# A recurrent attention loop with one PSUM bank for values and weighted values instead of two, and a fifth half-pair of weights kept in PSUM

## Chip, cores and metric

One NeuronCore of a Trainium2 chip. The time is the device time of one execution in microseconds; a lower one is better. Weights, activations and outputs are bf16 and matrix products accumulate in f32.

## What is computed

Two independent parts share a kernel and their outputs are put side by side. Part A is a gated long convolution (shift filter, FFT convolution over 2048 positions, gate). Part B is attention with a recurrent memory, and it takes most of the time:

```python
mem = mem0                                   # 8 rows
for s in range(n_seg):                       # 64 segments of 32 rows
    h = concat([mem, x[s*32:(s+1)*32]])      # 40 rows x 1024
    q, k, v = h @ Wq, h @ Wk, h @ Wv         # 32 heads of 128
    p = softmax(where(mask, q @ k.T * scale, -1e9))
    o = (p @ v) @ Wo                         # 40 rows x 1024
    mem = o[:8]                              # next segment's memory
    outs.append(o[8:])
```

Each segment needs the one before it, because its first eight rows are that one's result. `Wq`, `Wk`, `Wv` and `Wo` are 1024 x 4096 (or the reverse) each, 32 MB in all, and every segment uses every weight once.

## The kernel before

**Where weights are.** The weights are cut into 64 pairs of 512 KB, a pair being two tiles of 128 x 1024: 8 pairs of q and k in each of four groups of eight heads (`("qk", g, i)`), 4 of v and 4 of the output projection o. Most pairs are resident in SBUF for the whole loop. Two are "parked" in PSUM (`PARKED`): four banks hold their four tiles, and in each segment ACT copies one tile and DVE the other into a buffer of the ring (`unpark`, lines 715 to 719). The other 17 (`STREAM`) are copied once into DRAM tiles `Wst` in a convenient layout and then read anew in every segment. They go through `wring`, a ring of five buffers of 512 KB. `done` (line 724) is called behind the last product with a pair; it hands the freed buffer to the next pair of the list, either by a DMA that SP issues (`place`, line 707) or by an entry on the list of copies out of PSUM. SP issues in program order, so a load waits until PE has finished with the buffer, and the loads behind it wait too.

**PSUM.** A bank is 2 KB in each of 128 partitions. During the loop four of the eight banks hold parked weights, one (`ps_qk`) takes the sums of q and k and later those of the output, two (`ps_acc`) take in turn the sums of v (`vacc`), the weighted values (`otacc`), the transposed `x` and a filler, and one (`ps_ts`) takes the transposed q and k, the scores and the transposed memory.

**A segment.** Line 906 starts the loop. For each group g from 0 to 3: `qk_part` multiplies 32 rows (eight of memory and 24 of `x`; the last eight of every segment's `x` do not depend on the memory and were multiplied before the loop) by eight chunks of q and k weights, each chunk four matmuls of 512 columns side by side in four column strips of the array. `scores` and `softmax` belong to the group before (g - 1), and `pv` (lines 836 to 856), the weighted values, to the one before that (g - 2). `pv` has four parts c, each with four small matmuls that use 32 rows of the array (tile position 32c), one PSUM bank, and a cast by ACT from that bank into `OT` (line 851). It is called for two parts at a time. Then `qk_out` casts q and k on ACT, `v_part` multiplies by the v weights, `tr_a` transposes q and k, and `v_out` casts v. After the four groups, the output products `wo` follow (eight steps of four matmuls for each group), with group 3's softmax and the weighted values of groups 2 and 3 between them, the transposition of the next segment's `x` (`h_rows`) and at last `Y_sb`, an ACT cast of the output. `fill_mem` transposes its first eight rows into the next `hT`, and the next segment starts.

**Queues around it.** ACT works in order: copies out of PSUM, the casts, the exponentials and, in group 2, the issue of the load of the next `x` rows, `H` (line 661). `H` shares its buffer with `Y_sb`, so that load waits until the stores of `Y_sb`, which POOL issues, have landed. DVE does the row maxima, the normalisation and the copies of transposed q and k. POOL copies the last eight rows of `OT` into `OL`, issues the stores of `OL` and `Y_sb`, and the loads of `VB`, the values made before the loop. Semaphores are placed by the framework; the order of instructions on each engine is the order of the program, written out by hand.

After the loop, the last stage (lines 969 on) multiplies the collected rows `OLs` by the output weights. In the last segment, the streamed o pairs are loaded into SBUF places that are no longer needed (lines 911 to 915).

Of the kernel before, what the change touches and what calls it, by code (L numbers as in the profile page):

```python
# [21 lines left out]
def fused_kernel(ctx: ExitStack, tc, q, k, v, shift_k, ssm_k, ssm_D, outa, x, mem0, Wq, Wk, Wv, Wo, outb, n_seg):  # L22
# [15 lines left out]
    scale = 128.0 ** -0.5  # L38
    RING = 5
    STREAM = {"qk": ((2, 5), (3,), (2, 6), (2, 6)), "v": ((0, 3), (1,), (2,), (2,)), "o": ((2,), (1,), (0, 3), (2,))}  # L40
    PARKED = {("qk", 0, 2): ("v", 0, 1), ("v", 0, 3): ("qk", 1, 6)}

    msched = tc.manual_schedule()
# [13 lines left out]
    streamed = [key for key in pairs if key[2] in STREAM[key[0]][key[1]]]  # L57
    parked = list(PARKED.values())
    resident = [key for key in pairs if key not in streamed and key not in parked]
    Wst = {key: dram.tile([128, 2, 1024], BF, name=f"Wst{key[0]}{key[1]}_{key[2]}") for key in streamed}  # L60

    def half_src(key, n):
        m, g, i = key
# [51 lines left out]
    def relay(n):  # L115

        for _ in range(n):
            if relaid:
                key = relaid.pop(0)
                for i in range(2):  # L120
                    nc.gpsimd.dma_start(Wst[key][:, i, :], half_src(key, i))

    relaid = list(streamed)
# [540 lines left out]
    H = load_h(0)  # L664


    ps_park = cw_.enter_context(tc.tile_pool(name="b_ps_park", bufs=1, space=PSUM))
    park = {key: [ps_park.tile([128, 1024], BF, name=f"park{key[1]}_{n}") for n in range(2)] for key in parked}

    park_s = stv.tile([128, 4, 1024], BF, tag="stv", name="park_s")  # L670
    halves = [(key, n) for key in parked for n in range(2)]
    assert rows.at >= 160
    rows.load_to(96)
    park_w = []
# [8 lines left out]
    for i, (key, n) in enumerate(halves):  # L683
        tw = ps_p.tile([128, 1024], BF, tag="pp", name="park_t")
        for c in range(8):
            nc.tensor.transpose(tw[:, c * 128:(c + 1) * 128], park_w[i][:, c * 128:(c + 1) * 128], ident[:])
        nc.vector.tensor_copy(park_s[:, i, :], tw[:])
        rows.half(2, "AD")
        for c in range(8):
            nc.tensor.transpose(park[key][n][:, c * 128:(c + 1) * 128], park_s[:, i, c * 128:(c + 1) * 128], ident[:])  # L690
    while rows.at < 192:
        rows.half(2, "AD")
    assert len(rows.loaded) == 96
# [3 lines left out]

    pp = ExitStack()
    ps_qk = pp.enter_context(tc.tile_pool(name="b_ps_qk", bufs=1, space=PSUM))
    ps_acc = pp.enter_context(tc.tile_pool(name="b_ps_acc", bufs=2, space=PSUM))  # L700
    ps_ts = pp.enter_context(tc.tile_pool(name="b_ps_ts", bufs=1, space=PSUM))

    placed = {}
# [3 lines left out]
    def place():  # L707

        if todo:
            key = todo.pop(0)  # L710
            t = ring.tile([128, 2, 1024], BF, tag="wring", name="wring")
            nc.sync.dma_start(t[:], Wst[key][:])
            placed.setdefault(key, []).append((t[:, 0, :], t[:, 1, :]))

    def unpark():
        while to_copy:
            key, t = to_copy.pop(0)
            nc.scalar.copy(t[:, 0, :], park[key][0][:])  # L718
            nc.vector.tensor_copy(t[:, 1, :], park[key][1][:])

    def pair(key):
        return (res[key][:, 0, :], res[key][:, 1, :]) if key in res else placed[key].pop(0)
# [18 lines left out]
    def qk_part(u, kcs):  # L741
        if kcs[0] == 0:
            u.qk = ps_qk.tile([128, 512], F32, tag="qk", name="qkacc")
        for kc in kcs:
            w = pair(("qk", u.g, kc))
            for t in range(2):
                for c2 in range(2):
                    p0 = 32 * (2 * t + c2)
                    nc.tensor.matmul(u.qk[p0:p0 + 32, :], lhsT=hT[:, kc, :], rhs=w[t][:, c2 * 512:(c2 + 1) * 512],  # L749
                                     start=(kc == 0), stop=(kc == 7), tile_position=(0, p0))  # L750
            done(("qk", u.g, kc))
# [84 lines left out]
    def pv(u, s, cs, ts_bank=False):  # L836
        if cs[0] == 0:
            u.OT = act2.tile([128, 8, 40], BF, tag="OT", name="OT")
        PTv = u.PT[:].rearrange("p (a i) k q -> p i k a q", a=2)
        for c in cs:  # L840
            pool, tag = (ps_ts, "ts") if ts_bank and c == 2 else (ps_acc, "acc")
            ot = pool.tile([128, 512], F32, tag=tag, name="otacc")
            r = slice(32 * c, 32 * c + 32)
            for i in range(2):
                o = ot[:, 64 * i:64 * i + 64]
                nc.tensor.matmul(o, lhsT=u.v[r, i * 128:(i + 1) * 128], rhs=PTv[r, i, 0], start=True, stop=False,  # L846
                                 tile_position=(32 * c, 0))
                nc.tensor.matmul(o, lhsT=VB[r, i * 128:(i + 1) * 128], rhs=PTv[r, i, 1], start=False, stop=True,  # L848
                                 tile_position=(32 * c, 0))
            ov = ot[:, 0:128].rearrange("e (i q) -> e i q", i=2)  # L850
            nc.scalar.copy(u.OT[:, 2 * c:2 * c + 2, :], ov[:, :, 0:40])  # L851
        if cs[-1] == 3:
            to = OL[:] if s + 1 < n_seg else OLs[:, s]
            nc.gpsimd.tensor_copy(to[:, 8 * u.g:8 * u.g + 8, :], u.OT[:, :, 32:40])  # L854
            if u.g == 3 and s + 1 < n_seg:
                nc.gpsimd.dma_start(OLd[s], OL[:].rearrange("e h r -> e (h r)"))

    def wo(u, Y, hhs=range(8)):
        for hh in hhs:
            if hh % 2 == 0:  # L860
                w = pair(("o", u.g, hh // 2))
            for dq in range(4):
                nc.tensor.matmul(Y[32 * dq:32 * dq + 32, 0:256], lhsT=u.OT[:, hh, 0:32],  # L863
                                 rhs=w[hh % 2][:, dq * 256:(dq + 1) * 256],
                                 start=(u.g == 0 and hh == 0), stop=(u.g == 3 and hh == 7),
                                 tile_position=(0, 32 * dq))
            if hh % 2 == 1:
                done(("o", u.g, hh // 2))
# [37 lines left out]
    for s in range(n_seg):  # L906
        us = []
        for g in range(4):
            if g == 2 and s + 1 < n_seg:
                H = load_h(s + 1)  # L910
            if g == 2 and s + 1 == n_seg:
                spare = [key for key in resident if key[0] != "o" and key[1] < 2 and key not in early]
                for key, at in zip([key for key in streamed if key[0] == "o"], spare):
                    nc.sync.dma_start(res[at][:], Wst[key][:])
                    res[key] = res[at]
            u = nxt
            us.append(u)
            qk_part(u, range(0, 4))
            unpark()
            if g < 3:  # L920
                nxt = load_b(s, g + 1)
            elif s + 1 < n_seg:
                nxt = load_b(s + 1, 0)
            if g >= 1:
                S = scores(us[g - 1])
            if g >= 2:
                pv(us[g - 2], s, (0, 1))
            if g >= 1:
                softmax(us[g - 1], S)
            qk_part(u, range(4, 6))  # L930
            if g >= 2:
                pv(us[g - 2], s, (2, 3))
            qk_part(u, range(6, 8))
            qk_out(u)
            v_part(u, range(0, 8))
            tr_a(u)
            v_out(u)
            unpark()
            if g == 3 and s + 1 == n_seg:
                for s0, s1 in ((0, 32), (32, s)):  # L940
                    nc.sync.dma_start(OLs[:, s0:s1].rearrange("e s h r -> e s (h r)"),
                                      OLd[s0:s1].rearrange("s e x -> e s x"))
        Y = ps_qk.tile([128, 512], F32, tag="qk", name="yacc")
        wo(us[0], Y, range(0, 4))
        softmax(us[3], scores(us[3]))
        wo(us[0], Y, range(4, 8))
        pv(us[2], s, (0, 1))
        wo(us[1], Y, range(0, 4))
        pv(us[2], s, (2, 3))
        wo(us[1], Y, range(4, 8))  # L950
        if s + 1 < n_seg:
            hT = new_hT()
            h_rows(H, hT, 8)
        wo(us[2], Y)
        pv(us[3], s, (0, 1))
        pv(us[3], s, (2, 3), True)
        if s + 1 < n_seg:
            load_vb(s + 1)
        wo(us[3], Y)
        Y_sb = act.tile([128, 256], BF, tag="st", name="Y_sb")  # L960
        nc.scalar.copy(Y_sb[:], Y[:, 0:256])
        if s + 1 < n_seg:
            fill_mem(hT, Y_sb)
            idle = ps_acc.tile([128, 512], F32, tag="acc", name="idle")
            keep_warm(idle, 2)
        for dq in range(4):
            nc.gpsimd.dma_start(outb[32 * s:32 * s + 24, dq * 256:(dq + 1) * 256], Y_sb[32 * dq + 8:32 * dq + 32, :])

    pp.close()
    ps_l = cw_.enter_context(tc.tile_pool(name="b_ps_l", bufs=2, space=PSUM))  # L970
    outl = outb.rearrange("(s t) d -> t s d", t=32)
    for sh in range(2):
# [83 lines left out]
```

## Time and profile before

| What | Value |
|---|---|
| Median of 3 runs | 2201.1 us (2187.66 to 2211.53) |
| Profiled execution | 2200.53 us, span 2198.5 us |
| First and last `Y_sb` | 448.0 and 2137.0 us |
| Busy in the span | PE 1808.6, PEld (weight loads) 1028.8, DVE 1082.4, ACT 836.0, POOL 500.4 us |
| Moved in the span | 732.29 MB, mean 333 GB/s |
| Streamed loads, 512 KB each | q and k 448, v 320, o 315; 6.2 to 6.3 us from issue to landing |
| Granted TensorE clock | 0.96 of full speed |

PE is TensorE, ACT ScalarE, DVE VectorE, POOL GpSimd, SP SyncE. In the views, "L851" is a line of the kernel, `out<-in` are the names of the tiles, and an arrow behind an idle time names what ended it; "issue" there means that the engine waited for nothing that the profile shows. A row of the order of time merges equal instructions that follow each other: start, duration, engine, line, operation, names, shapes, count. The end of a matmul is modelled, since matmuls are pipelined: starts are the better clock.

### The profile page before, as it was taken

Reading aid. Unit: us, or ns where it says so; the run is one execution under the profiler, and the core shown is the slowest. Engines: PE = TensorE matmul, PEld = TensorE weight load, DVE = VectorE, ACT = ScalarE, POOL = GpSimd, SP = SyncE. Lnnn points to the kernel's source line nnn. Section 1 sums busy time; section 2 is a strip of 40 time slices with the busy share of each in tenths; the row PEclk is TensorE's granted clock in tenths of the full one; section 3 lists DMA queues with packets and bytes.
Section 4 is the critical chain, followed back from the end, with each engine's and each line's share of the span. In section 5 each row is a group of like instructions: output and inputs, shape, how many; then the busy total and the mean of one; then the engine's idle time right before and its main releaser. Section 6 shows DMA issues by size and latency. Waiting matters only on the chain.

```text
span 2198.5 us, 88235 instructions
## 1 busy us (share of the span) xinstructions
PE 1808.6 (82%) x37779; PEld 1028.8 (47%) x37808; DVE 1082.4 (49%) x3235; ACT 836.0 (38%) x2538; POOL 500.4 (23%) x983
## 2 busy tenths in 40 slices
PE   4788877688888888788888878888888888888878
PEld 2332233354444445444544545544444445444558
DVE  6896822244544444444445445544444444444530
ACT  5456721133333334333333334333333333333320
POOL 4004622022222222222222222222222222222210
PEclk9999999899999999999999999999999999999999
DMA  7799889699999999999999999999999999999990
GB/s 255 267 353 350 302 302 369 248 354 345 343 341 365 344 358 367 339 342 333 349 352 361 365 357 364 364 345 353 358 353 347 349 347 361 323 348 345 357 328 21
DMA packets 275666, 732.29 MB, mean 333 GB/s; under 512 B 73323, under 2 KB 84539, under 8 KB 274761
## 3 DMA queue, kind: packets, MB, share of 16 engines
q1 hardware_dynamic: 242062, 683.06, 85.8%
q0 software_dynamic: 24320, 37.37, 5.2%
q10 hardware_dynamic: 8892, 6.23, 0.9%
q8 instruction: 295, 4.83, 0.9%
q14 instruction: 97, 0.79, 0.1%
HBM read 676.14 MB, written 59.18 MB: 334 GB/s over the span
## 4 chain that ended last, share of the span: by engine, by line
DMA 38%; PE 33%; issue 8%; DVE 3%; ACT 2%; POOL 1%; ACTq 1%; SPq 0%; POOLq 0%; DVEq 0%
PE qkacc L749 10%; DMA wring<-Wstv 10%; DMA wring<-Wstqk 8%; DMA wring<-Wsto 7%; PE yacc L863 6%; DMA out_dram<-Y_sb 5%; PE vacc L764 5%; DMA OLd<-OL 5%; PE otacc L846 3%; PE pl L979 3%; PE tp L777 2%; ACT OT L851 1%; PE otacc L848 1%; PE S L805 1%; DVE S L820 1%
## 5 line engine op out<-in xcount | busy, mean ns | idle before, releaser
L749 PE MATMUL qkacc<-Wqk,hT 128*32 128x512 bf16 x4096 | 354.6, 388 | 1.3 <-issue 1.3
L851 ACT CAST OT<-otacc 128x80 bf16<-128x80 f32 x1024 | 183.4, 233 | 438.6 <-PE otacc L848 391.2
L854 POOL COPY OL<-OT 128x64 bf16<-128x64 bf16 x252 | 63.3, 251 | 1221.9 <-ACT OT L851 1221.9
L764 PEld LDWEIGHTS <-hT 128*32 128x32 bf16 x8192 | 227.4, 98 | 190.1 <-issue 140.4
L749 PEld LDWEIGHTS <-hT 128*32 128x32 bf16 x8192 | 179.0, 98 | 215.4 <-issue 79.7
L863 PE MATMUL yacc<-Wo,OT 128*32 128x256 bf16 x5632 | 248.6, 278 | 22.2 <-issue 21.8
L863 PEld LDWEIGHTS <-OT 128*32 128x32 bf16 x8192 | 188.0, 97 | 103.5 <-issue 74.1
L764 PE MATMUL vacc<-Wv,hT 128*32 128x256 bf16 x5120 | 229.9, 279 | 2.7 <-issue 1.4
L749 PE MATMUL qkacc<-wring,hT 128*32 128x512 bf16 x2048 | 210.1, 398 | 24.3 <-DMA wring<-Wstqk 22.4
L764 PE MATMUL vacc<-wring,hT 128*32 128x256 bf16 x3072 | 145.4, 278 | 92.6 <-DMA wring<-Wstv 89.3
L846 PE MATMUL otacc<-PT,vsb 32*128 32x64 bf16 x2048 | 147.9, 192 | 55.3 <-ACT OT L851 49.1
L786 DVE COPY QT<-tp 128x256 bf16<-128x256 bf16 x256 | 74.7, 292 | 206.4 <-PE tp L777 198.8
L749 PE MATMUL qkacc<-Wearly,hT 128*32 128x512 bf16 x2048 | 171.0, 413 | 3.7 <-DVE hT L881 0.4
L718 ACT COPY wring<-park 128x1024 bf16<-128x1024 bf16 x128 | 129.9, 1015 | 110.4 <-PE qkacc L749 98.4
L755 ACT CAST qks<-qkacc 128x512 bf16<-128x512 f32 x256 | 150.5, 588 | 53.8 <-PE qkacc L749 48.6
L830 DVE TENSOR_REDUCE sm<-P 128x4 f32<-128x256 bf16 x256 | 107.6, 420 | 118.9 <-ACT P L828 118.9
L772 ACT CAST vsb<-vacc 128x256 bf16<-128x256 f32 x256 | 95.4, 373 | 179.2 <-PE vacc L764 178.2
L827 ACT ACTIVATE P<-S 128x128 bf16<-128x128 f32 x256 | 71.5, 279 | 238.3 <-DVE P L826 123.4
L819 DVE TENSOR_REDUCE mx<-S 128x4 f32<-128x160 f32 x256 | 83.2, 325 | 155.8 <-PE S L816 154.3
L863 PE MATMUL yacc<-wring,OT 128*32 128x256 bf16 x2520 | 131.5, 278 | 32.5 <-DMA wring<-Wsto 20.2
L798 POOL DMA_DIRECT2D VB<-VBd x256 | 152.3, 600 | 8.9 <-issue 3.6
L848 PE MATMUL otacc<-PT,VB 32*128 32x64 bf16 x2048 | 144.3, 188 | 8.9 <-issue 8.7
(218 smaller groups left out, 2830.0 us busy)
## 6 DMA issues: line engine op xcount, KB each, us to landing
wring<-Wstqk SPq DMA_DIRECT2D x448, 512.0 KB, 6.3
wring<-Wstv SPq DMA_DIRECT2D x320, 512.0 KB, 6.2
wring<-Wsto SPq DMA_DIRECT2D x315, 512.0 KB, 6.2
SK<-s_sb SPq DMA_DIRECT2D x8, 1024.0 KB
SU<-s_sb SPq DMA_DIRECT2D x8, 1024.0 KB, 5.4
QKBd<-stq POOLq DMA_DIRECT2D x4, 2048.0 KB, 9.8
Kg<-SK SPq DMA_DIRECT2D x16, 512.0 KB, 6.0
Ug<-SU SPq DMA_DIRECT2D x16, 512.0 KB, 8.0
```

The source lines that it names most:

```text
L718: nc.scalar.copy(t[:, 0, :], park[key][0][:])
L749: nc.tensor.matmul(u.qk[p0:p0 + 32, :], lhsT=hT[:, kc, :], rhs=w[t][:, c2 * 512:(c2 + 1) * 512], start=(kc == 0), stop=(kc == 7), tile_pos ...
L755: nc.scalar.copy(u.qks[:], u.qk[:])
L764: nc.tensor.matmul(u.vacc[32 * c:32 * c + 32, 0:256], lhsT=hT[:, kc, :], rhs=w[kc % 2][:, c * 256:(c + 1) * 256], start=(kc == 0), stop=(k ...
L772: nc.scalar.copy(u.v[:], u.vacc[:, 0:256])
L798: nc.gpsimd.dma_start(VB[32 * c:32 * c + 32, :], VBd[8 * s:8 * s + 8].rearrange("r (g c x) -> c g r x", g=4, c=4)[c])
L819: nc.vector.tensor_reduce(out=mx[:], in_=S[:], op=ALU.max, axis=AX.X)
L830: nc.vector.tensor_reduce(out=sm[:], in_=P[:], op=ALU.add, axis=AX.X)
L846: nc.tensor.matmul(o, lhsT=u.v[r, i * 128:(i + 1) * 128], rhs=PTv[r, i, 0], start=True, stop=False, tile_position=(32 * c, 0))
L848: nc.tensor.matmul(o, lhsT=VB[r, i * 128:(i + 1) * 128], rhs=PTv[r, i, 1], start=False, stop=True, tile_position=(32 * c, 0))
L851: nc.scalar.copy(u.OT[:, 2 * c:2 * c + 2, :], ov[:, :, 0:40])
L863: nc.tensor.matmul(Y[32 * dq:32 * dq + 32, 0:256], lhsT=u.OT[:, hh, 0:32], rhs=w[hh % 2][:, dq * 256:(dq + 1) * 256], start=(u.g == 0 and ...
```

## The change

One of the two banks of `ps_acc` is given to weights. It holds the second tile of the pair `("o", 1, 1)`, called `HALF`. That pair was streamed whole; now its first tile alone is streamed, as a DMA of 256 KB into the ring, and ACT copies the other tile from PSUM into the same ring buffer. So 16.5 pairs a segment are streamed instead of 17.

`vacc`, `otacc`, the transposed `x` and the filler now use the one bank that is left. `pv` is called for one part at a time, and each part stands between other products: behind chunk 0, behind the scores, behind chunks 4 and 5 and behind chunk 6 in groups 2 and 3, and after each two steps of `wo` for group 2's parts. For group 3's parts, after the transposition of `x`, bank `ps_ts` is used in turn with `ps_acc`. `h_rows` moves to the middle of group 2's output products, and the load of `qkb` behind the scores. Before the loop one more tile is transposed twice into PSUM, and one tile less is copied into DRAM.

```diff
+    HALF = ("o", 1, 1)
...
     park = {key: [ps_park.tile([128, 1024], BF, name=f"park{key[1]}_{n}") for n in range(2)] for key in parked}
+    park[HALF] = [None, ps_park.tile([128, 1024], BF, name="park_half")]
...
-    ps_acc = pp.enter_context(tc.tile_pool(name="b_ps_acc", bufs=2, space=PSUM))
+    ps_acc = pp.enter_context(tc.tile_pool(name="b_ps_acc", bufs=1, space=PSUM))
...
-            nc.sync.dma_start(t[:], Wst[key][:])
+            if key == HALF:
+                nc.sync.dma_start(t[:, 0, :], Wst[key][:, 0, :])
+                to_copy.append((key, t))
+            else:
+                nc.sync.dma_start(t[:], Wst[key][:])
...
+            if key == HALF:
+                nc.scalar.copy(t[:, 1, :], park[key][1][:])
+            else:
+                nc.scalar.copy(t[:, 0, :], park[key][0][:])
+                nc.vector.tensor_copy(t[:, 1, :], park[key][1][:])
...
-            pool, tag = (ps_ts, "ts") if ts_bank and c == 2 else (ps_acc, "acc")
+            pool, tag = (ps_ts, "ts") if ts_bank else (ps_acc, "acc")
...
-            qk_part(u, range(0, 4))
+            qk_part(u, range(0, 1))
+            if g >= 2:
+                pv(us[g - 2], s, (0,))
+            qk_part(u, range(1, 4))
             unpark()
+            if g >= 1:
+                S = scores(us[g - 1])
             if g < 3:
                 nxt = load_b(s, g + 1)
             elif s + 1 < n_seg:
                 nxt = load_b(s + 1, 0)
-            if g >= 1:
-                S = scores(us[g - 1])
             if g >= 2:
-                pv(us[g - 2], s, (0, 1))
+                pv(us[g - 2], s, (1,))
+            qk_part(u, range(4, 6))
+            if g >= 2:
+                pv(us[g - 2], s, (2,))
             if g >= 1:
                 softmax(us[g - 1], S)
-            qk_part(u, range(4, 6))
+            qk_part(u, range(6, 7))
             if g >= 2:
-                pv(us[g - 2], s, (2, 3))
-            qk_part(u, range(6, 8))
+                pv(us[g - 2], s, (3,))
+            qk_part(u, range(7, 8))
...
-        pv(us[2], s, (0, 1))
-        wo(us[1], Y, range(0, 4))
-        pv(us[2], s, (2, 3))
-        wo(us[1], Y, range(4, 8))
+        for c in range(4):
+            wo(us[1], Y, range(2 * c, 2 * c + 2))
+            pv(us[2], s, (c,))
+        wo(us[2], Y, range(0, 4))
         if s + 1 < n_seg:
             hT = new_hT()
             h_rows(H, hT, 8)
-        wo(us[2], Y)
-        pv(us[3], s, (0, 1))
-        pv(us[3], s, (2, 3), True)
+        wo(us[2], Y, range(4, 8))
+        for c in range(4):
+            pv(us[3], s, (c,), c % 2 == 1)
```

More of the change, by code (lines that the diff above doesn't have):

```diff
@@ L59, in fused_kernel @@
     resident = [key for key in pairs if key not in streamed and key not in parked]
-    Wst = {key: dram.tile([128, 2, 1024], BF, name=f"Wst{key[0]}{key[1]}_{key[2]}") for key in streamed}
+    Wst = {key: dram.tile([128, 1 if key == HALF else 2, 1024], BF, name=f"Wst{key[0]}{key[1]}_{key[2]}")
+           for key in streamed}
     def half_src(key, n):
@@ L119, in relay @@
                 key = relaid.pop(0)
-                for i in range(2):
+                for i in range(1 if key == HALF else 2):
                     nc.gpsimd.dma_start(Wst[key][:, i, :], half_src(key, i))
@@ L664, in fused_kernel @@
     H = load_h(0)
-    ps_park = cw_.enter_context(tc.tile_pool(name="b_ps_park", bufs=1, space=PSUM))
+    pk = ExitStack()
+    ps_park = pk.enter_context(tc.tile_pool(name="b_ps_park", bufs=1, space=PSUM))
     park = {key: [ps_park.tile([128, 1024], BF, name=f"park{key[1]}_{n}") for n in range(2)] for key in parked}
+    park[HALF] = [None, ps_park.tile([128, 1024], BF, name="park_half")]
     park_s = stv.tile([128, 4, 1024], BF, tag="stv", name="park_s")
-    halves = [(key, n) for key in parked for n in range(2)]
+    halves = [(key, n) for key in parked for n in range(2)] + [(HALF, 1)]
     assert rows.at >= 160
@@ L686, in fused_kernel @@
             nc.tensor.transpose(tw[:, c * 128:(c + 1) * 128], park_w[i][:, c * 128:(c + 1) * 128], ident[:])
-        nc.vector.tensor_copy(park_s[:, i, :], tw[:])
+        nc.vector.tensor_copy(park_s[:, i % 4, :], tw[:])
         rows.half(2, "AD")
         for c in range(8):
-            nc.tensor.transpose(park[key][n][:, c * 128:(c + 1) * 128], park_s[:, i, c * 128:(c + 1) * 128], ident[:])
+            nc.tensor.transpose(park[key][n][:, c * 128:(c + 1) * 128], park_s[:, i % 4, c * 128:(c + 1) * 128], ident[:])
     while rows.at < 192:
@@ L717, in unpark @@
             key, t = to_copy.pop(0)
-            nc.scalar.copy(t[:, 0, :], park[key][0][:])
-            nc.vector.tensor_copy(t[:, 1, :], park[key][1][:])
+            if key == HALF:
[3 more added lines that the diff above has]
+                nc.vector.tensor_copy(t[:, 1, :], park[key][1][:])
     def pair(key):
@@ L913, in fused_kernel @@
                 for key, at in zip([key for key in streamed if key[0] == "o"], spare):
-                    nc.sync.dma_start(res[at][:], Wst[key][:])
+                    if key == HALF:
+                        nc.sync.dma_start(res[at][:, 0, :], Wst[key][:, 0, :])
+                        nc.scalar.copy(res[at][:, 1, :], park[key][1][:])
+                    else:
+                        nc.sync.dma_start(res[at][:], Wst[key][:])
                     res[key] = res[at]
@@ L969, in fused_kernel @@
     pp.close()
+    pk.close()
     ps_l = cw_.enter_context(tc.tile_pool(name="b_ps_l", bufs=2, space=PSUM))
```

## The prediction

> **What bounds the kernel now.** I read the share of the chain of waits first, then the loop over segments alone, then who the tensor engine waits for in it, and last the order of time around the value products. The chain of waits by engine, the group of end-of-segment casts, and two windows (length; busy time and instruction count of PE, PEld, DVE, ACT, POOL; granted clock, DMA share, GB/s):
>
> ```profile
> DMA 38%; PE 33%; issue 8%; DVE 3%; ACT 2%; POOL 1%; ACTq 1%; SPq 0%; POOLq 0%; DVEq 0%
> ...
> L961 ACT CAST Y_sb<-yacc x64: 372/372/373, 448.0 to 2137.0; 128x256 bf16<-128x256 f32 x64
> ...
> 448.00:2137.00 1689.00, 1414.02 (x34648) 828.02 (x34649) 811.18 (x2771) 632.57 (x2206) 377.86 (x819) 0.97 0.98 351
> 100.00:200.00 100.00, 82.77 (x374) 32.96 (x380) 80.88 (x124) 54.88 (x83) 15.39 (x17) 0.93 0.94 336
> ```
>
> `Y_sb` ends a segment, so 63 segments take 1689.0 us: 26.81 us each. In them the DMA engines are busy 98% of the time, 26.3 us a segment, and PE 84%, 22.4 us. DMA sets the pace, but narrowly. How narrowly is told by what PE itself waits for between 448 and 2137 us (us in all, times, longest):
>
> ```profile
> PE vacc L764 <- DMA wring<-Wstv: 69.8, 95, 6.0
> PE otacc L846 <- ACT OT L851: 48.5, 118, 2.3
> PE yacc L863 <- issue: 32.1, 37, 1.8
> PE mt_tp L888 <- ACT Y_sb L961: 30.0, 63, 0.5
> PE qkacc L749 <- DMA wring<-Wstqk: 22.4, 45, 1.7
> PE yacc L863 <- DMA wring<-Wsto: 20.2, 26, 2.4
> ```
>
> Waiting for weights is 69.8 + 22.4 + 20.2 = 112.4 us, 1.78 us a segment. Without it PE would still need 26.81 - 1.78 = **25.03 us**, against 26.3 us of DMA. So whatever lengthens PE's own path by more than about 1.3 us a segment, less if DMA gets shorter, turns the bound over.
>
> **The change, part by part.** *Bytes.* One of 17 streamed pairs a segment becomes half a pair: 262,144 bytes fewer. The loop moves 351 GB/s at a share of 0.98, 358 GB/s at full share, so 0.73 us a segment less, and DMA needs 25.5 us. The half moves in rows of 2 KB where a pair moves in rows of 4 KB; in the window from 100 to 200 us, where most loads are 256 KB in 2 KB rows, 336 GB/s at 0.94 is 357 GB/s, so I give the half no surcharge. The Trainium skill (DMA: Bandwidth & Descriptors, Anatomy of one DMA) puts a fixed part of about 2 us on every transfer and charges bytes at 436 GB/s beside it: by that the half would save 0.60 us. The full-share rates above, alike for both sizes, do not show such a part in the queue's pace.
>
> *Entries into the value products.* The products of `pv` use 32 rows of the array, their neighbours 128. Around them, in group 3 of a segment (PE alone; start, us, line, names, shape, count):
>
> ```profile
> 1214.99 0.21 PE L816 MATMUL S<-KT,qkb 128*8 128x40 bf16 x8
> 1215.14 0.21 PE L846 MATMUL otacc<-PT,vsb 32*128 32x64 bf16 x2
> ...
> 1215.37 0.61 PE L749 MATMUL qkacc<-Wqk,hT 128*32 128x512 bf16 x8
> 1215.91 0.21 PE L846 MATMUL otacc<-PT,vsb 32*128 32x64 bf16 x2
> ...
> 1216.14 0.40 PE L749 MATMUL qkacc<-wring,hT 128*32 128x512 bf16 x4
> 1216.37 0.39 PE L749 MATMUL qkacc<-Wqk,hT 128*32 128x512 bf16 x4
> ```
>
> A chunk of q and k costs 0.22 us (1216.14 to 1216.37). Two from 1215.37 would let the next start at 1215.80; it starts at 1216.14. So this pair of parts, eight matmuls, costs 0.34 us, of which 0.11 is the entry (1215.80 to 1215.91). A part alone, below, is followed by the next product after 0.20 us (1224.28 to 1224.48), so it costs 0.11 + 0.20 = 0.31 us: what is paid for is going in and out, not the products. Now a segment has six pairs (groups 0 and 1 as they are done in groups 2 and 3, group 2 among the output products), 6 x 0.33 = 1.98 us (the one among the output products: eight matmuls from 1219.17, at 0.11 a step the next at 1219.39, in fact at 1219.72). After it has twelve single parts, 12 x 0.31 = 3.72 us. That is **+1.74 us** a segment on PE with no wait at all. If the price belonged to each part and not to each entry, it would be zero. The Trainium skill (TensorEngine Tiling (Array Packing), Key Properties) says that changing the tiling mode, not merely the tile, drains the engine: it speaks for the price per entry, and against this change.
>
> *The turn of the one bank.* A part's bank has to be copied out by ACT before the next part may write it (ACT rows, then PE rows):
>
> ```profile
> 1220.27 0.36 ACT L851 CAST OT<-otacc 128x80 bf16<-128x80 f32 x2
> 1220.86 0.36 ACT L851 CAST OT<-otacc 128x80 bf16<-128x80 f32 x2 [0.23 <-PE otacc L848]
> ```
> ```profile
> 1220.55 0.18 PE L846 MATMUL otacc<-PT,vsb 32*128 32x64 bf16 x1 [0.21 <-ACT OT L851]
> ...
> 1224.28 0.18 PE L846 MATMUL otacc<-PT,vsb 32*128 32x64 bf16 x1 [0.34 <-ACT OT L851]
> ...
> 1224.48 0.29 PE L863 MATMUL yacc<-Wo,OT 128*32 128x256 bf16 x4
> ```
>
> From a cast's start to the next part 0.28 us (1220.27 to 1220.55), from a part's start to its cast 0.31 (1220.55 to 1220.86): 0.59 us from part to part. In groups 2 and 3 after the change, part 1 and part 2 have two chunks between them (0.20 + 0.43 + 0.11 = 0.74, no wait), part 2 and 3 one (0.53, wait 0.06), and part 3 and the first value projection, which now needs the same bank, one (0.42, wait 0.17): 0.23 x 2 = 0.46. Among the output products two steps lie between parts, 0.53 us, so 0.06 twice; but part 0's cast also stands behind the softmax on ACT, whose second exponential starts at 1220.19 here: cast at 1220.27, part 1 at 1220.55, while PE would be there at 1219.49 + 0.22 (part 0 enters after two steps more) + 0.20 + 0.22 + 0.11 = 1220.24: 0.31. Together 0.43, less the 0.21 that the second pair waits now: +0.22. For group 3's own parts after the last transposition of `x`, two waits stand where one was: +0.10. The extra copy of 1.01 us (the row of `wring<-park` has 1015 ns) lies on ACT at the end of group 2, behind the cast of values, and delays group 3's first cast until part 1 is 0.04 late; DVE is not touched. Sum **+0.82 us**; bounds 0.4 (if group 2 and 3 hide half) and 1.2.
>
> *Behind the load of H.* In group 2 ACT first issues the load of `H`, which waits for the stores of the last `Y_sb`, and everything of ACT is queued behind it:
>
> ```profile
> 1211.00 0.55 ACTq L661 DMA_DIRECT2D H<-in_B_x_dram  x1
> 1211.64 0.35 ACT L851 CAST OT<-otacc 128x80 bf16<-128x80 f32 x2 [1.98 <-PE otacc L848]
> ...
> 1211.91 0.18 PE L846 MATMUL otacc<-PT,vsb 32*128 32x64 bf16 x1 [0.43 <-ACT OT L851]
> ```
>
> Now the first part that needs a cast comes 2.2 us into the group; after, part 1 comes at 1.44 (four chunks, scores, part 0), 0.77 earlier, and stands that much longer. Not every segment has H this late: 0 to 0.77, I take **+0.4**.
>
> *What gives back.* PE waits for no engine ("issue") 52 us in the loop, 0.83 us a segment. A slower PE asks for code later, and 295 instruction packets share the DMA engines: nothing here shows how much, so 0 to -0.83, **-0.4**.
>
> *At nothing.* The order on SP keeps its count of loads; the load of `qkb` moves behind the scores that it waits for already. The fifth parked piece costs sixteen transposes and a copy before the loop, while PE waits 19.58 us for `wring<-Wstv` at 429.69; one relayed half disappears there. Without that cover it is 1 to 2 us once.
>
> **Sum.** 25.03 + 1.74 + 0.82 + 0.4 - 0.4 = 27.59 us of PE against 25.5 of DMA: PE becomes the bound. 27.59 - 26.81 = +0.78 us; x 63 = +49 us on the profiled execution's 2200.5 (0.6 below the median of 2201.1): **2250 us**.
>
> **Rivals.** *DMA stays the bound, faster.* Entries priced by the part and turns hidden: PE's path grows under 0.5 us, and 63 x 0.73 = 46 us go: 2155. For it: DMA's share of 0.98. Against: single parts cost 0.31 in the rows. Chance 0.12. By the 0.60 us of the Trainium skill's page on DMA it would be 2163.
>
> *Gains and costs meet.* The turns and the H stall fall into waits that are there anyway, only the entries stay: 25.03 + 1.74 = 26.77, 2198. For it: PE's 1.78 us of slack and 0.83 of issue. The Trainium skill (TensorE: Matmul & The Clock Gate, HAM oscillation) reports a kernel in which a second PSUM buffer gained nothing more; the 48.5 us of waits for `OT` with two banks speak against it here. Chance 0.14.
>
> *H decides, much slower.* H is tied to the last `Y_sb` (10.5 us after the cast at 1200.53), not to PE. If waits for weights vanish in groups 0 and 1, PE reaches group 2 up to 1 us sooner and stands there: 28.4 us, +100, 2300. It decides once group 2 starts 9 us after `Y_sb` or sooner. Chance 0.14.
>
> **Numbers.** The forecast has 0.60. All costs at their low end (0.4 for turns, no H, issue gone) give 25.03 + 1.74 + 0.4 - 0.83 = 26.34, DMA then near; at their high end 25.03 + 1.74 + 1.2 + 0.77 = 28.7. The range 2185 to 2300 leaves out the faster case and a little beyond the slowest. About 1% is what a measurement here can tell: faster 0.12, same 0.14, slower 0.74.
>
> **What would show it.** DMA share in the loop falls to about 0.92; PE's waits for `wring` fall well under 1 us a segment; waits for `OT` at the value products and at the first value projection grow to 1.5 us or more; PE rows show each part with its own gap before and after. If the DMA share stays at 0.97 or more and `Y_sb` comes every 26.1 us, the sum is wrong at the entries.

## The result and the profile after

| | before | after |
|---|---|---|
| Median | 2204.1 us (4 runs, 2187.7 to 2211.5) | 2276.3 us (4 runs, 2269.2 to 2289.9) |
| Ratio after to before, 95% interval | | 1.034 (1.030 to 1.038) |
| Profiled execution, its span | 2200.5, 2198.5 us | 2269.2, 2267.1 us |
| One segment of the loop | 26.81 us | 27.83 us |
| Granted clock in the loop, DMA share, GB/s | 0.97, 0.98, 351 | 0.98, 0.95, 329 |

The changed kernel is 3.4% slower, 26 us beyond the forecast of 2250 and inside its range. Of the changed kernel, first the share of the chain of waits by engine; then two groups, the end-of-segment casts and the new copy out of the fifth bank; then the window of the loop (length; busy time and count of PE, PEld, DVE, ACT, POOL; granted clock, DMA share, GB/s):

```profile
PE 40%; DMA 28%; issue 10%; DVE 3%; ACT 3%; POOL 2%; ACTq 1%; POOLq 0%; SPq 0%; DVEq 0%
```
```profile
L982 ACT CAST Y_sb<-yacc x64: 372/372/526, 452.6 to 2206.1; 128x256 bf16<-128x256 f32 x64
...
L727 ACT COPY wring<-park_half 128x1024 bf16<-128x1024 bf16 x63 | 64.2, 1019 | 0.0
```
```profile
452.60:2206.10 1753.50, 1509.62 (x34652) 880.56 (x34656) 814.41 (x2771) 720.40 (x2268) 374.22 (x819) 0.98 0.95 329
```

PE has taken DMA's place at the head of the chain (40% against 28%; it was 33% against 38%). The two end casts give 1753.5 us for 63 segments. The new copy does what it says, once in a segment, 1.02 us, and ACT stood idle for nothing before it. PE is busy 95.6 us longer in the loop than before (1509.6 against 1414.0) and idle 31 us less. What it waits for in the loop (us in all, times, longest):

```profile
PE otacc L857 <- ACT OT L862: 95.8, 174, 4.4
PE vacc L775 <- DMA wring<-Wstv: 75.7, 97, 3.8
...
PE qkacc L760 <- DMA wring<-Wstqk: 18.9, 38, 1.5
...
PE yacc L874 <- issue: 0.9, 2, 0.5
```

Against before: waits for `OT` have doubled (48.5 to 95.8 us), the waits for values' weights are as long as they were (69.8 to 75.7), and the output products wait neither for code (32.1 to 0.9) nor for their streamed weights (20.2 us before, not in the list after).

Group 2 of a segment of the changed kernel in order of time, PE first, then ACT:

```profile
1244.44 0.20 PE L857 MATMUL otacc<-PT,vsb 32*128 32x64 bf16 x1
...
1245.43 0.21 PE L827 MATMUL S<-KT,qkb 128*8 128x40 bf16 x8
1245.99 0.18 PE L857 MATMUL otacc<-PT,vsb 32*128 32x64 bf16 x1 [0.34 <-ACT OT L862]
```
```profile
1245.06 0.56 ACTq L663 DMA_DIRECT2D H<-in_B_x_dram  x1
1245.71 0.23 ACT L862 CAST OT<-otacc 128x80 bf16<-128x80 f32 x1 [1.45 <-PE S L827]
1246.30 0.23 ACT L862 CAST OT<-otacc 128x80 bf16<-128x80 f32 x1 [0.36 <-PE otacc L859]
```

Part 0 is multiplied at 1244.44 and could be cast 0.31 us later. ACT casts it at 1245.71, behind the issue of `H`, which ends at 1245.62. PE has done the scores and stands until part 1 may write the bank at 1245.99. From there part 1's cast follows part 0's at 0.59 us, the turn that the prediction took from the rows of before. What holds the issue of `H`, and ACT's casts behind it, are the stores of `Y_sb`. ACT's waits that end with their landing, in the loop before and after:

```profile
ACT OT L851 <- DMA out_dram<-Y_sb: 39.3, 12, 4.5
```
```profile
ACT OT L862 <- DMA out_dram<-Y_sb: 70.8, 22, 5.5
```

Group 3 has no `H`; its first product and its first value projection:

```profile
1249.24 0.40 PE L760 MATMUL qkacc<-Wqk,hT 128*32 128x512 bf16 x4
...
1252.66 0.60 PE L775 MATMUL vacc<-Wv,hT 128*32 128x256 bf16 x13
```

3.42 us between them. I measured this stretch in every segment, and two others, from PE's rows (shortest and mean of the 63 segments, us; the last column is the changed kernel with `H` issued by POOL, of which more below):

| Stretch | before | after | after, `H` by POOL |
|---|---|---|---|
| group 2, first q and k product to first value projection | 2.62, 3.42 | 3.42, 4.77 | 3.42, 3.79 |
| group 3, the same | 2.62, 2.89 | 3.42, 3.48 | 3.42, 3.45 |
| first output product to the first one behind group 3's weighted values | 5.32, 6.46 | 6.11, 6.19 | 6.09, 6.36 |
| rest of the segment, mean | 14.04 | 13.39 | 13.18 |

Each stretch has become longer at its shortest: by 0.80, 0.80 and 0.79 us (four more steps of 0.11, moved ahead of the transposition of `x`, don't count: the third stretch holds them before and after). The 0.79 is the least sure of the three, since a single segment of before is as short as 5.32. But among the output products the mean has fallen by about 0.3. There PE used to wait for code and weights (52.3 us in the loop), and those waits are gone. Group 2 has grown by 1.35 us, far more than its 0.80; that is where `H` stands.

### The profile page after: what moved, and what is told of

The parts are those of the page before. It is cut to its first block, busy times and chain, and to the rows that moved or that the text cites. A ratio compares the mean times of both kernels' runs of the same rounds, so it can differ in the third digit from the quotient of the medians.

```text
span 2267.1 us, 88487 instructions
## 1 busy us (share of the span) xinstructions
PE 1910.5 (84%) x37824; PEld 1082.9 (48%) x37824; DVE 1086.8 (48%) x3236; ACT 925.8 (41%) x2602; POOL 496.2 (22%) x982
## 4 chain that ended last, share of the span: by engine, by line
PE 40%; DMA 28%; issue 10%; DVE 3%; ACT 3%; POOL 2%; ACTq 1%; POOLq 0%; SPq 0%; DVEq 0%
PE qkacc L760 12%; DMA out_dram<-Y_sb 11%; DMA OLd<-OL 10%; PE vacc L775 7%; PE otacc L857 6%; PE yacc L874 5%; DMA wring<-Wstv 4%; PE pl L1001 2%; PE tp L788 2%; PE otacc L859 2%; DMA wring<-Wstqk 2%; ACT OT L862 2%; ACTq L663 1%; DVE mx L830 1%; DVE S L831 1%
## 5 line engine op out<-in xcount | busy, mean ns | idle before, releaser
L862 ACT CAST OT<-otacc 128x80 bf16<-128x80 f32 x1024 | 219.8, 227 | 475.8 <-PE otacc L859 328.3
L760 PE MATMUL qkacc<-Wqk,hT 128*32 128x512 bf16 x4096 | 382.2, 394 | 0.0
L857 PE MATMUL otacc<-PT,vsb 32*128 32x64 bf16 x2048 | 235.8, 191 | 107.8 <-ACT OT L862 96.4
L775 PEld LDWEIGHTS <-hT 128*32 128x32 bf16 x8192 | 227.4, 99 | 189.7 <-issue 143.6
L760 PEld LDWEIGHTS <-hT 128*32 128x32 bf16 x8192 | 185.0, 95 | 193.1 <-issue 43.8
L857 PEld LDWEIGHTS <-vsb 32*128 32x128 bf16 x2048 | 143.8, 92 | 207.3 <-issue 170.7
L859 PE MATMUL otacc<-PT,VB 32*128 32x64 bf16 x2048 | 232.3, 189 | 0.3 <-DMA VB<-VBd 0.3
L760 PE MATMUL qkacc<-wring,hT 128*32 128x512 bf16 x2048 | 204.4, 387 | 20.7 <-DMA wring<-Wstqk 18.9
L841 DVE TENSOR_REDUCE sm<-P 128x4 f32<-128x256 bf16 x256 | 107.5, 420 | 202.3 <-ACT P L839 202.3
L859 PEld LDWEIGHTS <-VB 32*128 32x128 bf16 x2048 | 145.6, 93 | 103.5 <-issue 102.5
L874 PEld LDWEIGHTS <-OT 128*32 128x32 bf16 x8192 | 172.4, 96 | 34.6 <-issue 2.3
L760 PE MATMUL qkacc<-Wearly,hT 128*32 128x512 bf16 x2048 | 156.2, 382 | 4.6 <-DVE hT L892 0.4
```

Source lines behind the costliest of these rows:

```text
L775: nc.tensor.matmul(u.vacc[32 * c:32 * c + 32, 0:256], lhsT=hT[:, kc, :], rhs=w[kc % 2][:, c * 256:(c + 1) * 256], start=(kc == 0), stop=(k ...
L841: nc.vector.tensor_reduce(out=sm[:], in_=P[:], op=ALU.add, axis=AX.X)
```

## Experiments

The question: of the loss, how much is the price of single parts (entries), how much the one bank (turns), how much ACT standing behind `H`, and what do the saved bytes bring back? The rivals were: entries dominate; the bank dominates; `H` dominates. Ratios are to the kernel before, run beside each, with 95% intervals.

**The new order with two banks and 17 whole pairs.** Against the kernel before, the parts are single and the rest of the new order is kept (`h_rows` and the load of `qkb` moved, group 3's parts in turn in `ps_ts`); banks and bytes are those of before. The edit of the changed kernel:

```diff
-    HALF = ("o", 1, 1)
+    HALF = None
...
-    ps_acc = pp.enter_context(tc.tile_pool(name="b_ps_acc", bufs=1, space=PSUM))
+    ps_acc = pp.enter_context(tc.tile_pool(name="b_ps_acc", bufs=2, space=PSUM))
```

> The order of the changed kernel (value products one part at a time), but with two banks for values and weighted values and all 17 pairs streamed whole; nothing of the computation is left out. Theory, the entries cost: six more entries a segment put 1.74 us on PE with no turn of a bank in it; less the 0.8 us of waits for code that a slower PE loses, PE's own path is 25.03 + 1.74 - 0.8 = 26.0 us beside DMA's 26.3, and two paths of nearly one length do not fit into each other: about 27.2 us a segment, 2225 us (2210 to 2245). Rival, the turn of the one bank is what costs: with two banks 2204 us within 10.

Measured: 2207.9 us, 1.005 (1.001 to 1.009): 11 us above the kernel before. By its time this is the rival's case (2204 within 10), and it lies below the theory's range of 2210 to 2245. The price of an entry is there nevertheless. Group 3's stretch is 3.23 us at its shortest against 2.62, +0.61 for two more entries, where the prediction had 4 x 0.31 - 2 x 0.33 = 0.58. Among the output products, with no wait for a bank (PE rows of this kernel):

```profile
1244.27 0.20 PE L856 MATMUL otacc<-PT,vsb 32*128 32x64 bf16 x1
...
1244.48 0.40 PE L873 MATMUL yacc<-wring,OT 128*32 128x256 bf16 x8
1244.82 0.20 PE L856 MATMUL otacc<-PT,vsb 32*128 32x64 bf16 x1
```

0.55 us from part to part with two steps of 0.11 between: 0.33 us a part. That a change of tiling mode drains the engine, as the Trainium skill (TensorEngine Tiling (Array Packing), Key Properties) says, agrees with this +0.61 for the same sixteen products cut into four parts instead of two. So the price was right, and yet only 11 us of the 1.74 x 63 = 110 us reach the end. PE's busy time in the loop grew by 55 us (1469.2 against 1414.0) and its idle time fell by 48 (275.0 to 227.3), so a good part of the price lies where PE waited before. The clock, too, was at half for 68 us of this loop and for 106 of before's. What took the rest is not shown.

**Half a pair less with two banks.** The order and the banks of before; the half that would lie in the fifth bank is copied from a resident tile. The kernel so leaves out one tile of the output weights and uses another one twice:

```diff
+    HALF = ("o", 1, 1)
...
-            nc.sync.dma_start(t[:], Wst[key][:])
+            if key == HALF:
+                nc.sync.dma_start(t[:, 0, :], Wst[key][:, 0, :])
+                to_copy.append((key, t))
+            else:
+                nc.sync.dma_start(t[:], Wst[key][:])
...
-            nc.scalar.copy(t[:, 0, :], park[key][0][:])
-            nc.vector.tensor_copy(t[:, 1, :], park[key][1][:])
+            if key == HALF:
+                nc.scalar.copy(t[:, 1, :], res[("o", 1, 0)][:, 1, :])
+            else:
+                nc.scalar.copy(t[:, 0, :], park[key][0][:])
+                nc.vector.tensor_copy(t[:, 1, :], park[key][1][:])
```

> The kernel before, two banks and its own order, but the pair (o, 1, 1) is streamed as a half, and ACT copies its other tile into the ring from a resident tile in SBUF instead of from PSUM; so one tile of the output weights is another one's, and bytes, copies and order are what is measured. Theory, DMA sets the pace before the change: 0.73 us x 63 = 46 us less, 2158 us. Rival, PE waits for weights because they are wanted in bursts and not because there are too many of them: the waits stay as they did in the changed kernel (1.53 us a segment), 2190 to 2204 us.

Measured: 2178.2 us, 0.990 (0.983 to 0.997). By the ratio 0.9896 that is 23 us of 2201, half of the 46 that the bytes at full rate are worth, and between the two expectations (2158, and 2190 to 2204). What takes the other half is taken up again with `H` by POOL.

**One bank, 17 whole pairs.** The changed kernel without its gain:

```diff
-    HALF = ("o", 1, 1)
+    HALF = None
...
-    park[HALF] = [None, ps_park.tile([128, 1024], BF, name="park_half")]
```

> The changed kernel with its one bank and its order, but all 17 pairs streamed whole and no fifth tile in PSUM; nothing of the computation is left out. Theory, PE sets the pace after the change: the bytes are worth little, 2276 to 2295 us. Rival, DMA still counts in full beside PE: 2276 + 46 = 2322 us.

Measured: 2281.7 us, 1.038 (1.029 to 1.047), as expected. In the changed kernel the half pair brings 5 us by the medians, 8 by the ratios, which these intervals can't tell from nothing; the 46 of the full rate lie outside them. Bytes alone no longer bound it.

**`H` issued later, still by ACT.** In the changed kernel the load is issued behind group 3's casts of q and k instead of at the start of group 2:

```diff
-            if g == 2 and s + 1 < n_seg:
-                H = load_h(s + 1)
...
             qk_out(u)
+            if g == 3 and s + 1 < n_seg:
+                H = load_h(s + 1)
```

> The changed kernel, but ACT issues the load of H in group 3, behind the cast of q and k, where the stores of Y_sb have long landed, and not at the start of group 2. Theory, ACT stands behind H and the one bank with it: the waits for OT in group 2 are about 59 us in the loop, so 2276 - 45 = 2231 us (2215 to 2250). Rival, the time that PE stands for H hides waits for weights that come out again: 2265 us or more.

Measured: 2236.3 us, 1.017 (1.009 to 1.025), as expected: 37 us gone by moving one instruction. PE's waits for `OT` fall from 95.8 to 37.3 us in the loop, and 26.4 us of waits for `H` itself come up before the transposition of `x`: it now arrives late.

**Pairs of parts with one bank.** The kernel before with `bufs=1` for `b_ps_acc`, nothing else:

```diff
-    ps_acc = pp.enter_context(tc.tile_pool(name="b_ps_acc", bufs=2, space=PSUM))
+    ps_acc = pp.enter_context(tc.tile_pool(name="b_ps_acc", bufs=1, space=PSUM))
```

> The kernel before with its own order, value products two parts at a time, and its 17 whole pairs, but one bank instead of two for values and weighted values; nothing of the computation is left out. Theory: the second part of each of six pairs now stands a whole turn, 0.59 us instead of 0.06, so about 3.2 us a segment in place of the 1.74 + 0.82 us of single parts; with H behind the one bank as in one_bank_whole_pairs (2282 us): 2282 + 0.7 x 63 = 2325 us (2300 to 2360). Rival, parting the pairs is the mistake: faster than 2282 us.

Measured: 2421.9 us, 1.101 (1.098 to 1.104), nearly twice the loss expected. The wait for `OT` and the loop of this kernel:

```profile
PE otacc L846 <- ACT OT L851: 237.6, 504, 3.4
```
```profile
452.40:2356.70 1904.30, 1557.63 (x34648) 912.30 (x34649) 814.90 (x2771) 675.18 (x2206) 374.30 (x819) 0.91 0.90 312
```

504 waits are eight in each of 63 segments. They cost 189 us more than before's 48.5. Other waits shrink meanwhile, for values' weights from 69.8 to 39.6 us, and those for code and for output weights are gone, so that PE is idle only 72 us longer than before (346.7 against 275.0). The other 144 us are busy time (1557.6 against 1414.0) for the same 34,648 products; the lower clock (below) may account for most of it. So with one bank the parts have to be spread out, and the spreading is worth more (10.1% against the 3.8% of single parts in one bank, both with 17 whole pairs) than its entries cost.

**`H` by POOL, in the kernel before:**

```diff
-            nc.scalar.dma_start(H_[:], xq[:, 32 * s - 8:32 * s + 24, :])
+            nc.gpsimd.dma_start(H_[:], xq[:, 32 * s - 8:32 * s + 24, :])
...
-            if g == 2 and s + 1 < n_seg:
+            if g == 3 and s + 1 < n_seg:
                 H = load_h(s + 1)
```

> The kernel before, two banks, its order and its 17 whole pairs, but POOL issues the load of H at the start of group 3, behind the landing of the stores of Y_sb, instead of ACT at the start of group 2. Theory, with two banks H costs little, since only the second pair stands behind it and DMA sets the pace: 2185 to 2197 us, the most being the 14 us of waits for OT in group 2. Rival, H costs as much as with one bank: 2157 us.

Measured: 2187.3 us, 0.993 (0.990 to 0.996), as expected: with two banks `H` on ACT costs 0.7%.

**The same in the changed kernel:**

> The changed kernel, its one bank and its single parts, with the load of H issued by POOL at the start of group 3 and nothing else. Theory: after_h_late (2236 us) still waited 0.42 us a segment for H's landing; without it 2236 - 27 = 2210 us (2200 to 2225), and what is left above the kernel before is entries and turns. Rival, ACT's issue of H cost nothing there: 2236 us within 8.

Measured: 2192.1 us, 0.997 (0.994 to 1.000): below the expected range of 2200 to 2225. `H` weighs more than I had thought. PE's wait for `OT` and the loop of this kernel:

```profile
PE otacc L857 <- ACT OT L862: 34.4, 113, 0.8
```
```profile
452.70:2140.00 1687.30, 1497.01 (x34652) 874.12 (x34656) 816.80 (x2771) 721.01 (x2268) 418.23 (x881) 0.99 0.98 341
```

The loop is 66.2 us shorter than that of the changed kernel (1753.5), and 61.4 us of it are gone from one line, the waits for `OT`. The longest falls from 4.4 to 0.8 us, and no wait of ACT ends with the stores of `Y_sb` any more (70.8 us above). In the table above, 0.98 us of group 2's mean goes, which is 62 us in 63 segments. One instruction moved, and one wait and one stretch shrink by nearly what the loop does. Between the medians the gain is larger, 84 us (82 by the ratios): the profiled execution of the changed kernel was its fastest run (2269.2), that of this one its slowest (2203.1).

**Half a pair less, two banks, `H` by POOL.** Both edits shown above on the kernel before, so again without one tile of the output weights:

> half_streamed_two_banks (its one tile of output weights is another one's, as there) with the load of H issued by POOL at the start of group 3: what the half pair would be worth if its bank cost nothing. Theory, DMA sets the pace of the kernel before and of before_h_pool (2187 us): 0.6 us of packets a segment less are at most 2187 - 38 = 2149 us, and since two banks showed 19 us of it, 2160 us (2150 to 2172). Rival, the bytes are worth nothing once H is out of the way, because bursts and not bytes make PE wait: 2182 us or more.

Measured: 2152.4 us, 0.979 (0.975 to 0.983), as expected. The half pair is now worth 31 us of 2201 (0.993 to 0.979), where with `H` on ACT it was 23; the intervals don't tell these two apart, so that `H` hid part of the gain is not shown. The packets in the traces fit the 31 rather than the 46: the DMA engines are busy 0.51 us a segment less (26.25 with `H` by POOL, 25.74 here), 32 us in 63 segments, not 0.73. On the queue of the weights (q1), rows of 2 KB took 101.5 ns in the mean, more than half of the 178.1 of rows of 4 KB, and these had taken 177.2 without the half. The prediction gave the half no surcharge from the stretch of 100 to 200 us, where rows of 2 KB do take half as long (92.7 against 185.5 ns); in the loop they don't. The largest wait for code and the loop:

```profile
PE yacc L871 <- issue: 39.4, 38, 2.5
```
```profile
448.20:2094.30 1646.10, 1389.52 (x34648) 822.12 (x34649) 810.96 (x2771) 692.20 (x2267) 421.75 (x881) 0.97 0.99 350
```

**Pairs again, with bank `ps_ts`.** Two trials keep one bank and the fifth piece, give `H` to POOL, and halve some entries again, by doing two parts at once, the second in the bank of transposed q and k. First among the output products alone (the last argument of `pv` names the parts in that bank):

```diff
...
-        for c in range(4):
-            wo(us[1], Y, range(2 * c, 2 * c + 2))
-            pv(us[2], s, (c,))
+        wo(us[1], Y, range(0, 4))
+        pv(us[2], s, (0, 1), (1,))
+        wo(us[1], Y, range(4, 8))
+        pv(us[2], s, (2, 3), (3,))
```

> The changed kernel, with the load of H as in before_h_pool, and group 2's value products among the output products two at a time again, the second of two in the bank that holds the scores, which are used up by then. Theory: after_h_late (2236 us) lost 0.4 us a segment to H's landing and spent 4.35 us to the transposition of x, of which two entries and the turns, 0.6 us, go: 1.0 x 63 = 63 us less at most, half of it where DMA is next: 2200 us (2175 to 2220). Rival, entries among the output products are hidden: 2236 - 26 = 2210 us or more.

Measured: 2181.7 us, 0.991 (0.988 to 0.994), inside the range expected. Then parts 0 and 1 of groups 2 and 3 as well, with parts 2 and 3 moved up to the scores and behind chunk 5:

```diff
-            qk_part(u, range(0, 1))
+            qk_part(u, range(0, 2))
             if g >= 2:
-                pv(us[g - 2], s, (0,))
-            qk_part(u, range(1, 4))
+                pv(us[g - 2], s, (0, 1), (1,))
+            qk_part(u, range(2, 4))
...
```

> As tail_pairs_h_pool, and in groups 2 and 3 parts 0 and 1 as a pair behind two chunks, part 1 in the bank of the transposed q and k, part 2 behind the scores, part 3 behind chunk 5 and the softmax behind it, so that no part stands for a turn. Theory: 3.42 us to the first value projection becomes 3.25, 0.17 x 2 x 63 = 21 us less at most; DMA with 16.5 pairs is near, as in half_streamed_two_banks (2178 us): 2185 us (2170 to 2200), so faster than both kernels if PE's path was all that cost the change its gain. Rival, nothing left to win on PE: as tail_pairs_h_pool within 5 us.

Measured: 2184.8 us, 0.993 (0.990 to 0.996): the number expected, but no step down from the first trial. The waits of the second say why:

```profile
PE S L816 <- DVE KT L798: 33.6, 61, 0.7
...
PE otacc L857 <- DVE KT L798: 29.1, 94, 0.6
```

Part 1's bank has to be emptied of transposed keys by DVE first, so the entries saved are paid with 62.7 us of waits for DVE (PE is busy 48 us less in the loop than in the first trial, and idle 40 us more). Both are faster than the kernel before, and neither can be told from the kernel before with `H` by POOL (0.993): the fifth piece with one bank earns nothing that these runs can show.

## Why the prediction was right, and where its terms were not

Four comparisons lead step by step from the kernel before to the changed one, in us of 2201 (their sum is the whole by construction):

| From, to | Ratio | us |
|---|---|---|
| before, then `H` by POOL | 1 to 0.9934 | -15 |
| then half a pair less | 0.9934 to 0.9793 | -31 |
| then one bank and single parts | 0.9793 to 0.9969 | +39 |
| then `H` back on ACT: the changed kernel | 0.9969 to 1.0340 | +82 |
| sum | | +75 |

The ends of each are uncertain by about 0.4%, some 9 us. The third step also moves the source of the copied half from SBUF to PSUM, `h_rows` and the load of `qkb`; by the profiled loops it is 41 us, and the last one 66.

*Direction and bound.* Right: the kernel became slower, PE leads its chain of waits, and the saved bytes are worth little there (5 to 8 us). Of the 0.78 us a segment forecast, 1.02 came. But the loss is not made up as forecast: entries and turns, 2.56 us a segment in the sum, cost 0.62 in the steps above, and `H`, 0.4 in the sum, cost 1.06 more than with two banks.

*The sum: two mistakes that nearly cancel.* It made PE's own path the whole segment, with no wait for weights left. In the trace of after, PE waits 95 us for `wring` in the loop, 1.50 us a segment, not "well under 1". And PE's own path is 27.83 - 1.50 = 26.33 us, +1.30 on 25.03, not +2.56. So 1.26 us too many on PE and 1.50 too few of waiting give 27.59 in place of 27.83: that the total came this near is luck. Waits for weights moved rather than vanished: those of the output products went (20.2 us), those of the values stayed. That SP's loads wait in order for buffers that PE frees is a reading that would explain it; it was not tried by itself.

*Entries, +1.74, and turns, +0.82.* The prices were right. In the shortest passages groups 2 and 3 are 0.80 us longer each, against 0.58 + 0.23 forecast (0.61 and 0.19, as the kernel with the new order and two banks splits them), and the output products 0.79; together 2.39 against 2.56. What was wrong was to count them all on the path. All of both, with the other moves of the third step, cost 39 us, 0.62 us a segment. Much of them fell into time in which PE had stood idle: from the kernel with half a pair less and `H` by POOL to the changed kernel with `H` by POOL, PE's busy time grows by 107.5 us (1389.5 to 1497.0) while its idle time falls by 66.3 (256.6 to 190.3), and the largest wait that goes is for code, 39.4 to 2.5 us.

*Waits for code, -0.4.* The bounds held (0 to -0.83), and the far one was right: 52 us fell to about 2. Nothing in the profile of before told that, and why they go is not shown.

*Behind the load of H, +0.4.* The term that was mis-sized. Its place and mechanism were right, its size was not: +67 us (82 with one bank, 15 with two), 1.06 us a segment, where 0.77 was the upper bound. (The profiled loops give 66.2 and 14.6, so 0.82.) Two things were missed. With two banks part of the stall lay beside other waits: group 2 gets 0.38 us shorter when `H` leaves ACT (mean 3.42 to 3.04), but the segment only 0.23, the rest comes up as waits elsewhere. With one bank, 0.98 of group 2 and 1.05 of the segment go. And the issue of `H` ends 2.3 us into group 2 on average (1.8 before), while part 1 wants the bank at about 1.44. The rival "H decides" named this stall; the time came midway between it and the forecast (2276 between 2250 and 2300), and the two were one case in two sizes. Its reason was another, though: that PE reaches group 2 up to 1 us sooner. PE's rows have group 2 start 9.46 us after the cast of `Y_sb` before and 9.33 after, 0.13 sooner, and 9 us or less behind it in 18 of 63 segments both times. Most of the difference is that the issue of `H` ends later, 11.6 us after the cast in place of 11.3; why is not shown.

*Bytes, 0.73 us a segment.* Worth 31 us of the 46 with two banks and `H` by POOL, 23 with `H` on ACT, 5 to 8 in the changed kernel. The rival of 2155 needed two banks: with them 2178 was measured, and 2152 only with `H` moved as well. The rival of 2198, costs hidden in waits, is near what the changed kernel with `H` by POOL does (2192). The Trainium skill's fit behind the prediction's 0.60 us (DMA: Bandwidth & Descriptors, Anatomy of one DMA) is given for transfers that GpSimd issues; these loads are issued by SP, and no run here tests it.

*What should have shown it.* Two of the four signs came: waits for `OT` are 1.52 us a segment, and each part has its own gap. Two did not: DMA share fell to 0.95, not 0.92, and the waits for `wring` stayed at 1.50 us a segment. That a second PSUM buffer gained nothing more in the kernel of the Trainium skill (TensorE: Matmul & The Clock Gate, HAM oscillation) does not carry over: here the second bank alone is worth 10.1% with the order of before.

## What to carry to other kernels

Price a change by its pieces in undisturbed passages, then ask for each piece which wait it lies beside: here 151 us of right prices (2.39 x 63) cost 39. Before a buffer's depth goes from two to one, look down the in-order queue of the engine that empties it for any instruction with a foreign wait (here a load that waits for stores), and move that first: it cost 82 us with one bank and 15 with two. And find such an instruction's worth by moving it alone.

## What was not expected of the hardware

The granted clock fell to 0.91 in the loop of the kernel with pairs and one bank (0.97 before). In the record of the clock it stands at half for 356 us of that loop, 106 us before and 82 us after, in stretches of multiples of 3.4 us. What is special there are 504 waits of PE averaging 0.47 us each. By an estimate from these figures, 250 us more at half clock are worth up to 125 us, which would cover the 97 us by which that kernel missed its forecast; that the waits cause the lower clock is argued, not tried. The Trainium skill (TensorE: Matmul & The Clock Gate, A second HAM failure mode: psum-queue depth-cycling) tells of a kernel that loses the clock to frequent micro-idles between groups of products; the waits and the clock of this kernel are in line with that.

The DMA engines' busy share did not fall with the bytes. The changed kernel moves 329 GB/s at a share of 0.95, which is 346 GB/s at full share, against 358 before. So the engines are busy 26.4 us a segment (0.95 x 27.83) with fewer bytes, and 26.3 before. In the traces each packet takes longer: on the queue of the weights, rows of 4 KB took 183.4 ns in the mean, against 176.9 before. Why they do is open.
